# Clustered attention with a token-mixing MLP: the order and the staging of the weight sums are changed

## The chip, the cores and the metric

The kernel runs on one core of a Trainium2 chip. The metric is the device time of one execution in microseconds (us). Five engines work side by side and are ordered by semaphores: PE (TensorE: matmuls and their weight loads), DVE (VectorE), ACT (ScalarE), POOL (GpSimd) and SP (SyncE, which here only issues DMAs). Each engine runs its instructions strictly in the order of the program: one that waits holds all that stand behind it on that engine. ACT issues some DMAs too. Matmul results are written to PSUM banks; everything else is in SBUF or in DRAM.

## The reference

```
q_assign = argmax(normalised q . normalised centroids);  k_assign likewise
scores   = where(q_assign == k_assign, q k^T / 8, -1e9);  attn = softmax(scores) v
x  = attn, heads joined                      # [4, 768, 512]
u  = x + (x^T U V)^T                         # rank-32 mix over the 768 tokens
out = u + relu(u w_ch1) w_ch2                # 512 -> 2048 -> 512, for each batch
```

There are 4 batches, 8 heads, 768 tokens, 64 values a head. U, V, w_ch1 and w_ch2 come as float64; the kernel gets their bits as int64.

## The kernel before

**Attention.** 16 items (4 batches by 4 pairs of heads) go through a software pipeline of 12 steps an item. `M0` is the step after the last item, where the MLP begins; times below are in steps after M0.

**The plan.** All work is cut into small functions (`gemm1`, `join`'s caller `load_weights`, `recover`, `store_sum`, ...). `at(time, fn, args)` puts each call into a list under a hand-chosen time; the list is sorted by it and run once, at build time. So a time is no time of the chip: it sets only the order in which instructions stand on each engine.

**The MLP in two ways.** Batch 0 is done directly, as two halves of 384 tokens (`nh = 2`) of 16 steps each: in step f, `gemm1` (12 matmuls, L598 to L600) multiplies by one 128-column slice of w1, `after_gemm1` (ACT L606, DVE L607) applies relu and splits the result into a high and a low float32r part, and `gemm2` (9 matmuls, L617 to L619) multiplies by the matching slice of w2, half a step to a step later. Every operand is held as a high and a low part, and three products stand for one. Batches 1 to 3 are done from step 32 on by a scheme with seven instead of eight block products (`seven1` L800 to L802, `seven2` L876 to L878). It needs, for w1 and w2 of each group, three blocks A11, A12, A22 and four sums of blocks S1 to S4. They are made once, beside batch 0, put into DRAM (`wc`) and fetched from there (`fetch_w1` L771, `fetch_w2` L783).

**Loading weights.** The weights are in four groups g of 512 columns, each with 4 pieces of w1 and 4 of w2, 128x512 each. Groups 0 and 1 are loaded during the attention. For groups 2 and 3 one piece is loaded in each of the steps 0 to 15: `fetch` (L151, a DMA of 512 KB on ACT's queue, two buffers), `upper` (ACT L159), `join` (DVE L169, L170, L172: the float32 is put together from the bits, in a PSUM bank of the pool that also serves gemm1 and the mix), then the high part (ACT L190) and the low part (DVE L191).

**A turn.** One turn makes the four sums of w1 or w2 of one group. `recover` adds high and low of a block again (ACT L659 copies the low part into the bank `ps_r`, DVE L660 adds the high part), `combine` (POOL L665 to L671) forms the sums, `split_high` (ACT L676) and `split_low` (POOL L680) split them, and `store_sum` (SP L684, L685) stores both parts. There are eight turns, in the order of the groups 0 to 3, 3.1 steps apart from step 3 on; the last begins at 26.3. `store_block` (SP L643) stores the plain blocks.

**Tokens.** u of a batch goes through DRAM (`u_scr`, stored in `mix_v`, L552). `fetch_u` and `turn_u` (PE transposes L587, ACT L589, DVE L590) bring the halves of batch 0, `fetch_half` (L738) and `turn_half` (L743) those of batch 1; `u_sums` and `u_halves` make the sums of token blocks for the seven products. `mix_u` (L533), `mix_sum` (L540 to L543) and `mix_v` (L549, L550) are the rank-32 mix; that of batch 3 lies in the first steps of the MLP.

Of the kernel before, what the change touches and what calls it, by code (L numbers as in the profile page):

```python
# [89 lines left out]
    "mix_u":    ( 18.88,  18.35,  18.48,  16.57),  # L90
    "mix_sum":  ( 19.11,   19.1,  19.15,  18.35),
    "mix_v":    (  20.5,   20.4,  20.68,  19.42),
}
# [24 lines left out]
def clustered_attention_moe(ctx: ExitStack, tc: tile.TileContext, qk, v, cen, moe_U, moe_V, w1, w2, out):  # L118
# [26 lines left out]

    def fetch(srcs, n, queue=nc.sync):

        step = srcs[0].shape[0]
        rw = raw.tile([P, 512], I64, name="rw")[0:step * len(srcs), 0:n]
        for i, src in enumerate(srcs):  # L150
            queue.dma_start(out=rw[i * step:(i + 1) * step], in_=src)  # L151
        return rw
# [9 lines left out]
    def join(rw, g, in_bank=False):  # L162


        r, n = rw.shape
        low = rw.bitcast(I32).rearrange("p (n two) -> p n two", two=2)[:, :, 0]
        b = work("ps_t").bitcast(I32)[0:r, 0:n]
        t = b if in_bank else raw.tile([P, 512], I32, name="rw_t")[0:r, 0:n]
        nc.vector.tensor_scalar(b, g, 3, None, op0=ALU.logical_shift_left)  # L169
        nc.vector.scalar_tensor_tensor(out=b, in0=g, scalar=-0x80000000, in1=b,  # L170
                                       op0=ALU.bitwise_and, op1=ALU.bitwise_or)
        nc.vector.scalar_tensor_tensor(out=t, in0=low, scalar=29, in1=b,  # L172
                                       op0=ALU.logical_shift_right, op1=ALU.bitwise_or)
        return rw, g, t
# [3 lines left out]
    def load_weights(g, step, stage):  # L178

        k, i = divmod(step, 4)  # L180
        if stage == 0:
            parts[g, step] = fetch([(w1, w2)[k][g, :, i, :]], 512, nc.scalar if g > 1 else nc.sync)
        elif stage == 1:
            parts[g, step] = upper(parts[g, step])
        elif stage == 2:
            parts[g, step] = join(*parts[g, step], g > 1)
        else:
            w = parts.pop((g, step))[2].bitcast(F32)
            hi, lo = wg[g][2 * k][:, i, :], wg[g][2 * k + 1][:, i, :]
            nc.scalar.copy(hi, w)  # L190
            (nc.vector if g > 1 or g == 1 and step in (1, 2, 3, 5) else nc.gpsimd).tensor_sub(lo, w, hi)  # L191

# [448 lines left out]
    def store_block(k, g, name, part):  # L641

        nc.sync.dma_start(out=wc[k][g][:, :, slot[k][name], part * 256:part * 256 + 256],  # L643
                          in_=blocks(k, g, part)[name].bitcast(F32))

    def temps(n):
        at = 3072 * (n % 2 == 0 or n > 5)
        return [pool["f"][:, at + 512 * j:at + 512 * j + 512].rearrange("p (a n) -> p a n", a=2) for j in range(4)]

    def high_of(n, j):  # L650
        f = pool["f"]
        places = [f[:, 5120:5632], f[:, 5632:6144], *pool["o"], f[:, 2048:2560], f[:, 2560:3072]]
# [37 lines left out]
    w1s = [w0.rearrange("p k i n -> p (k i n)")[:, 3584 * k:3584 * k + 3584] for k in range(2)]  # L690
    spare, count = [], {"bank": 0, "f": 0, "o": 0}

# [6 lines left out]
    def open_sevens():  # L699
# [6 lines left out]
        pool["st"] = rows.tile([P, HT, DM], F32, name="st", tag="R")  # L706
        ring = []
        for _ in range(2):
            ring += pieces(raw.tile([P, 512], I64, name="rw").bitcast(F32)[:, 0:768], HS)
        ring += [raw.tile([P, 512], F32, name="rw_g")[:, 0:HS] for _ in range(2)]  # L710
# [26 lines left out]
    def fetch_half(b, h):  # L737
        nc.sync.dma_start(out=pool["st"], in_=u_scr[b][:, h * HT:(h + 1) * HT, :])  # L738

# [268 lines left out]
    for b, (t_u, t_sum, t_v) in enumerate(zip(*mixes.values())):  # L1008
# [16 lines left out]
    at(M0 + 8.05, open_weights)  # L1025
# [10 lines left out]

    for n_, (g, k) in enumerate((g, k) for g in range(NG) for k in range(2)):
        c = M0 + (3 + 3.1 * n_ if n_ < 7 else 26.3)
        for r in range(4):
            at(c + 0.4 * r, recover, n_, k, g, r)  # L1040
            at(c + (0.9, 1.4, 1.75, 2.1)[r], combine, n_, r)
            at(c + (1.9, 2.25, 2.6, 2.8)[r], split_high, n_, r)
            at(c + (2.4, 2.7, 3.0, 3.3)[r], split_low, n_, r)
            at(c + (2.8, 3.1, 3.4, 3.7)[r], store_sum, n_, k, g, r)
# [96 lines left out]
```

## Time and profile before

| what | value |
|---|---|
| median of 3 runs | 1006.9 us (1006.17 to 1006.93) |
| the profiled execution | 1010.74 us, span 1008.9 us |
| mean granted clock of TensorE | 0.982 |
| PE busy | 954.8 us, 95% of the span |
| DVE busy | 713.3 us, 71% |
| POOL busy | 613.7 us, 61% |
| ACT busy | 471.9 us, 47% |
| first matmul of batch 0's MLP (step 0) | 466.9 us |
| its second half (step 16) | 557.4 us |
| first of the seven products (step 32) | 634.4 us |

Busy times are of the whole span; shares in single stages differ. The view of waits says for an engine which line waited for what (line waiting <- engine and line that released it), with the total, the number and the longest. Rows of a timeline have the start, the length, the engine, the line, the operation, what it writes and reads, and in brackets the idle time ahead of it with its releaser. `SPq` and `ACTq` are DMA issues. In the view of windows, the last four columns are the granted clock, the mean share of the 16 DMA engines that was busy, and GB/s.

### The profile page before, as it was taken

Reading aid. Unit: us, or ns where it says so; the run is one execution under the profiler, and the core shown is the slowest. Engines: PE = TensorE matmul, PEld = TensorE weight load, DVE = VectorE, ACT = ScalarE, POOL = GpSimd, SP = SyncE. Lnnn points to the kernel's source line nnn. Section 1 sums busy time; section 2 is a strip of 40 time slices with the busy share of each in tenths; the row PEclk is TensorE's granted clock in tenths of the full one; section 3 lists DMA queues with packets and bytes.
Section 4 is the critical chain, followed back from the end, with each engine's and each line's share of the span. In section 5 each row is a group of like instructions: output and inputs, shape, how many; then the busy total and the mean of one; then the engine's idle time right before and its main releaser. Section 6 shows DMA issues by size and latency. Waiting matters only on the chain. (4 is left out here: it accounts for less than half of the span.)

```text
span 1008.9 us, 15372 instructions
## 1 busy us (share of the span) xinstructions
PE 954.8 (95%) x5368; PEld 779.5 (77%) x5368; DVE 713.3 (71%) x1315; ACT 471.9 (47%) x837; POOL 613.7 (61%) x460
## 2 busy tenths in 40 slices
PE   6899999999999999988989998899999999999997
PEld 3565665676666766656767888799999999999997
DVE  5797776777787767676788523765788766877766
ACT  4454555565555545464455534443444433453330
POOL 5466676889678867753356845732357723866333
PEclk8899999999999999989999998999999999999999
DMA  6754653656575645346476994876667696676744
GB/s 182 193 130 118 163 147 94 201 155 158 144 227 155 152 116 147 98 132 231 142 234 229 312 350 180 315 275 241 256 237 274 221 377 239 227 280 252 261 147 146
DMA packets 76158, 205.28 MB, mean 203 GB/s; under 512 B 8561, under 2 KB 42865, under 8 KB 71217
## 3 DMA queue, kind: packets, MB, share of 16 engines
q1 hardware_dynamic: 73392, 195.82, 60.5%
q10 hardware_dynamic: 2688, 8.49, 2.7%
q8 instruction: 42, 0.69, 0.3%
q14 instruction: 36, 0.29, 0.1%
HBM read 131.07 MB, written 41.94 MB: 171 GB/s over the span
## 5 line engine op out<-in xcount | busy, mean ns | idle before, releaser
L442 DVE TENSOR_REDUCE m<-ps_max 128x1 f32<-128x384 f32 x384 | 195.3, 548 | 82.9 <-PE ps_max L440 81.2
L479 POOL TENSOR_TENSOR T<-T,pr 128x768 f32<-128x768 f32 x120 | 225.9, 1882 | 45.8 <-ACT pr L469 19.5
L469 ACT ACTIVATE pr<-st 128x768 f32<-128x768 f32 x192 | 154.6, 813 | 85.9 <-PE st L466 69.2
L440 PE MATMUL ps_max<-arena 128*128 128x384 f32 x384 | 127.1, 382 | 6.6 <-DVE oh L356 2.5
L487 PE MATMUL o_ps<-pr,vt 128*64 128x384 f32 x768 | 132.6, 495 | 0.1
L464 PE MATMUL st<-arena 128*128 128x384 f32 x384 | 105.2, 355 | 2.1 <-ACT pr L469 2.1
L440 PEld LDWEIGHTS ps_max<-arena 128*128 128x128 f32 x384 | 70.9, 193 | 45.1 <-issue 21.4
L487 PEld LDWEIGHTS o_ps<-pr,vt 128*64 128x64 f32 x768 | 52.9, 138 | 66.6 <-issue 60.3
L466 PE MATMUL st<-arena 97*128 97x384 f32 x384 | 99.6, 341 | 4.5 <-DMA arena<-mT 2.7
L479 POOL TENSOR_TENSOR T<-pr 128x768 f32<-128x768 f32 x30 | 56.5, 1883 | 65.1 <-ACT pr L469 65.1
L464 PEld LDWEIGHTS st<-arena 128*128 128x128 f32 x384 | 66.2, 190 | 18.1 <-issue 9.9
L466 PEld LDWEIGHTS st<-arena 97*128 97x128 f32 x384 | 70.3, 190 | 6.5 <-issue 4.6
L800 PE MATMUL ps_p<-arena,w 128*128 128x384 f32 x186 | 62.7, 337 | 2.8 <-DMA w<-wc 2.8
L491 ACT COPY os<-o_ps 128x384 f32<-128x384 f32 x32 | 15.4, 480 | 105.1 <-PE o_ps L487 105.1
L801 PE MATMUL ps_p<-arena,w 128*128 128x384 f32 x186 | 62.8, 338 | 0.2 <-POOL arena L767 0.2
L802 PE MATMUL ps_p<-arena,w 128*128 128x384 f32 x186 | 62.5, 336 | 0.0
L800 PE MATMUL ps_q<-arena,w 128*128 128x384 f32 x150 | 50.5, 337 | 0.0
L801 PE MATMUL ps_q<-arena,w 128*128 128x384 f32 x150 | 50.3, 336 | 0.0
L802 PE MATMUL ps_q<-arena,w 128*128 128x384 f32 x150 | 50.3, 335 | 0.0
L380 POOL TENSOR_TENSOR arena<-R,arena 128x768 fp32r<-128x768 f32 x18 | 34.5, 1921 | 13.6 <-ACT arena L375 8.0
L665 POOL TENSOR_TENSOR f<-f 128x512 f32<-128x512 f32 x8 | 10.3, 1294 | 53.1 <-DVE f L660 53.1
L607 DVE SCALAR_TENSOR_TENSOR hx<-ps_h,hx 128x384 fp32r<-128x384 f32 x32 | 17.7, 554 | 29.3 <-ACT hx L606 29.2
(527 smaller groups left out, 2454.6 us busy)
## 6 DMA issues: line engine op xcount, KB each, us to landing
w<-wc SPq DMA_DIRECT2D x24, 1024.0 KB
w<-wc SPq DMA_DIRECT2D x24, 768.0 KB
arena<-wc SPq DMA_DIRECT2D x20, 768.0 KB
wc<-f SPq DMA_DIRECT2D x52, 256.0 KB
R<-in_qk SPq DMA_DIRECT2D x32, 384.0 KB
arena<-arena SPq DMA_DIRECT2D x32, 384.0 KB
arena<-arena SPq DMA_DIRECT2D x64, 192.0 KB
arena<-wc SPq DMA_DIRECT2D x10, 1024.0 KB
```

The costliest lines, as they stand in the source:

```text
L380: eng.tensor_sub(part(X2[i % 3], 0, h), live["R", i][:, 2 * h:2 * h + 2].rearrange("p j q -> p (j q)"), part(X1[i % 3], 0, h))
L440: nc.tensor.matmul(ps[:, 0:HS], x1[:, 0, g // 2, g % 2, t * P:(t + 1) * P], x1[:, 1, h, g % 2, :], start=True, stop=True)
L442: nc.vector.reduce_max(live["m2", i][:, h, u:u + 1], ps[:, 0:HS], axis=AX.X)
L464: nc.tensor.matmul(st[:, j, 0:HS], x1[:, 1, hk, j, ks], x1[:, 0, h, j, :], start=True, stop=False)
L466: nc.tensor.matmul(st[:, j, 0:HS], x2[0:97, 1, hk, j, ks], x2[0:97, 0, h, j, :], start=False, stop=True)
L469: nc.scalar.activation(pr, st[:, :, 0:HS], AF.Exp, scale=SCALE)
L479: eng.tensor_add(T, live["p", i, h, 0] if c == 1 else T, live["p", i, h, c])
L487: nc.tensor.matmul(o_ps[64 * j:64 * j + 64, 0:HS], vv[:, c, j, :], pr[:, j, :], start=(c == 0), stop=(c == NT - 1))
L607: nc.vector.scalar_tensor_tensor(out=hl, in0=ps[:, 0:HS], scalar=0.0, in1=hh, op0=ALU.max, op1=ALU.subtract)
L800: nc.tensor.matmul(ps, w[:, 0, k], u[:, 0, k], start=(k == 0), stop=False)
L801: nc.tensor.matmul(ps, w[:, 0, k], u[:, 1, k], start=False, stop=False)
L802: nc.tensor.matmul(ps, w[:, 1, k], u[:, 0, k], start=False, stop=(k == 1))
```

## The change

- The order of the turns becomes groups 2, 3, 0, 1 (`turns_of`). For the first four, `recover` is left out: a new fifth stage of `load_weights`, `keep_joined`, copies the joined weights on ACT from the bank straight into the turn's scratch in `f`. Turns begin at 2.8, 6.8, 10.8, 14.8, 17.5, 20.0, 22.7 and 26.4; of the last, everything after `recover` comes 5.9 steps later.
- The stages of a load are spread: the fetch 2.6 steps ahead of the step (for the first two pieces 4.6), `upper` 1.45, `join` 0.45, high part 0.02, low part 0.0, `keep_joined` 0.53 behind. All fetches go on SP's queue. Every third piece goes into a third buffer in `f`.
- `join` of these groups uses the bank `ps_r`, one buffer, instead of the shared pool.
- `mix_sum` of batch 3 comes 0.7 steps earlier; its `mix_v` one tile each 0.45 steps instead of three at once. `turn_u(0)` is spread from step -7 on, `turn_half(1, h)` comes 3.8 and 2.0 steps earlier, `u_sums` of batch 1 1.1. `fetch_half(1, 1)` goes on ACT's queue, at 22.5 instead of 25.6. B11's subtraction in `u_halves` of batch 1 moves from POOL to DVE.
- Blocks of groups 2 and 3 are stored from step 4.6 on instead of 15.5. `fetch_w1` of the first two pairs moves from 23 and 26 to 24.5 and 28, `fetch_w2` to 30 through 32.2.

```
-    "mix_sum":  ( 19.11,   19.1,  19.15,  18.35),
-    "mix_v":    (  20.5,   20.4,  20.68,  19.42),
+    "mix_sum":  ( 19.11,   19.1,  19.15,  17.65),
+    "mix_v":    (  20.5,   20.4,  20.68,  18.42),
...
-    "g2":   ( -1.25,      0,    0.4,    0.7),
-    "g3":   (  6.75,      8,    8.4,    8.7),
+    "g2":   (  -2.6,  -1.45,  -0.45,  -0.02,   0.0,   0.53),
+    "g3":   (   5.4,   6.55,   7.55,   7.98,   8.0,   8.53),
...
-        b = work("ps_t").bitcast(I32)[0:r, 0:n]
+        b = (pool["y"].tile([P, 512], F32, name="ps_r") if in_bank else work("ps_t")).bitcast(I32)[0:r, 0:n]
...
-            parts[g, step] = fetch([(w1, w2)[k][g, :, i, :]], 512, nc.scalar if g > 1 else nc.sync)
+            spare_rw = None
+            if g > 1 and (8 * g + step) % 3 == 0:
+                spare_rw = pool["f"][:, 2048:3072].bitcast(I64)
+            parts[g, step] = fetch([(w1, w2)[k][g, :, i, :]], 512, nc.sync, spare_rw)
...
-            w = parts.pop((g, step))[2].bitcast(F32)
             hi, lo = wg[g][2 * k][:, i, :], wg[g][2 * k + 1][:, i, :]
-            nc.scalar.copy(hi, w)
-            (nc.vector if g > 1 or g == 1 and step in (1, 2, 3, 5) else nc.gpsimd).tensor_sub(lo, w, hi)
+            if stage == 3:
+                w = parts[g, step][2].bitcast(F32)
+                nc.scalar.copy(hi, w)
+            if stage == 5:
+                keep_joined(turns_of.index((g, k)), i, parts.pop((g, step))[2].bitcast(F32))
+            if stage == 4 or stage == 3 and g < 2:
+                w = parts[g, step][2].bitcast(F32)
+                eng = nc.vector if g > 1 or g == 1 and step in (1, 2, 3, 5) else nc.gpsimd
+                eng.tensor_sub(lo, w, hi)
...
+    turns_of = [(2, 0), (2, 1), (3, 0), (3, 1), (0, 0), (0, 1), (1, 0), (1, 1)]
+    def keep_joined(n, i, w):
+        at = 3072 * (n % 2 == 0)
+        f = pool["f"][:, at:at + 2048].rearrange("p (c k a n) -> p c k a n", c=2, k=2, a=2)
+        to = f[:, i // 2, :, i % 2] if n % 2 else f[:, :, 1 - i // 2, i % 2]
+        nc.scalar.copy(to, w.rearrange("p (c n) -> p c n", c=2))
...
-        return places[count["o"] % (6 if n < 6 else 4)].rearrange("p (a n) -> p a n", a=2)
+        return places[count["o"] % (4 if n < 7 else 2)].rearrange("p (a n) -> p a n", a=2)
...
-        nc.sync.dma_start(out=pool["st"], in_=u_scr[b][:, h * HT:(h + 1) * HT, :])
+        (nc.scalar if b == 1 and h else nc.sync).dma_start(out=pool["st"], in_=u_scr[b][:, h * HT:(h + 1) * HT, :])
...
-            at(o + t_v + (t if b < B - 1 else t // HT), mix_v, b, t)
+            at(o + t_v + (t if b < B - 1 else 0.45 * t), mix_v, b, t)
...
-                at(step + pace * k + (M0 if g else 0), load_weights, g, k, stage)
+                ahead = 2 if g == 2 and stage == 0 and k < 2 else 0
+                at(step + pace * k + (M0 if g else 0) - ahead, load_weights, g, k, stage)
...
-            at(m + (-4.5 + d if i else -1.52), turn_u, i, d)
+            at(m + (-4.5 + d if i else -7 + 0.6 * d), turn_u, i, d)
...
-        c = M0 + (3 + 3.1 * n_ if n_ < 7 else 26.3)
+        c = M0 + (2.8, 6.8, 10.8, 14.8, 17.5, 20.0, 22.7, 26.4)[n_]
+        if n_ > 3:
+            for r in range(4):
+                at(c + 0.3 * r, recover, n_, k, g, r)
+        wait = 5.9 if n_ == 7 else 0
...
+                since = (95, 142, M0 - 9, M0 - 2.5, M0 + 4.6, M0 + 10.6, M0 + 16.4, M0 + 19.7)[2 * g + k]
+                at(since + (6, 0.9, 1, 0.55)[g] * x, store_block, k, g, name, half)
...
-            fetched, turns = (o - 13.9, o - 6.4), (o - 7.7, o - 5.4)
+            fetched, turns = (o - 13.9, o - 9.5), (o - 11.5, o - 7.4)
...
-            at(M0 + 23 + 3 * K, fetch_w1, K, s0, s1)
-            at(M0 + (30.5 + 0.5 * K if s0 == 0 else 31.8 + 0.1 * K), fetch_w2, K, *range(s0, s1))
+            at(M0 + 24.5 + 3.5 * K, fetch_w1, K, s0, s1)
+            at(M0 + (30 + 0.7 * K if s0 == 0 else 31.5 + 0.7 * K), fetch_w2, K, *range(s0, s1))
```

More of the change, by code (lines that the diff above doesn't have):

```diff
@@ L144, in clustered_attention_moe, with fetch @@
     u_scr = [dram.tile([P, NT, DM], F32, name=f"u_scr{b}") for b in range(B)]
-    def fetch(srcs, n, queue=nc.sync):
+    def fetch(srcs, n, queue=nc.sync, rw=None):
         step = srcs[0].shape[0]
-        rw = raw.tile([P, 512], I64, name="rw")[0:step * len(srcs), 0:n]
+        if rw is None:
+            rw = raw.tile([P, 512], I64, name="rw")[0:step * len(srcs), 0:n]
         for i, src in enumerate(srcs):
@@ L644, in store_block @@
                           in_=blocks(k, g, part)[name].bitcast(F32))
+    turns_of = [(2, 0), (2, 1), (3, 0), (3, 1), (0, 0), (0, 1), (1, 0), (1, 1)]
[4 more added lines that the diff above has]
+        nc.scalar.copy(to, w.rearrange("p (c n) -> p c n", c=2))
     def temps(n):
         at = 3072 * (n % 2 == 0 or n > 5)
-        return [pool["f"][:, at + 512 * j:at + 512 * j + 512].rearrange("p (a n) -> p a n", a=2) for j in range(4)]
+        x = pieces(pool["f"][:, at:at + 2048], 512) if n != 5 else pool["wide"]
+        return [x[j].rearrange("p (a n) -> p a n", a=2)
+                for j in ((1, 0, 3, 2) if n % 2 else range(4))]
     def high_of(n, j):
         f = pool["f"]
-        places = [f[:, 5120:5632], f[:, 5632:6144], *pool["o"], f[:, 2048:2560], f[:, 2560:3072]]
+        places = [f[:, 5120:5632], f[:, 5632:6144], *pool["o"]]
         count["o"] += 1
-        return places[count["o"] % (6 if n < 6 else 4)].rearrange("p (a n) -> p a n", a=2)
+        return places[count["o"] % (4 if n < 7 else 2)].rearrange("p (a n) -> p a n", a=2)
     def recover(n, k, g, j):
@@ L690, in clustered_attention_moe @@
     w1s = [w0.rearrange("p k i n -> p (k i n)")[:, 3584 * k:3584 * k + 3584] for k in range(2)]
-    spare, count = [], {"bank": 0, "f": 0, "o": 0}
+    spare, count = [], {"bank": 0, "f": 3, "o": 0}
     def pieces(x, n):
@@ L706, in open_sevens @@
         pool["st"] = rows.tile([P, HT, DM], F32, name="st", tag="R")
-        ring = []
+        ring, pool["wide"] = [], []
         for _ in range(2):
-            ring += pieces(raw.tile([P, 512], I64, name="rw").bitcast(F32)[:, 0:768], HS)
+            x = raw.tile([P, 512], I64, name="rw").bitcast(F32)
+            ring += pieces(x[:, 0:768], HS)
+            pool["wide"] += pieces(x, 512)
         ring += [raw.tile([P, 512], F32, name="rw_g")[:, 0:HS] for _ in range(2)]
@@ L721, in open_right @@
         pool["acc"] = {key: acc[k // 2][:, k % 2] for k, key in enumerate((B11, T1, T3, T2))}
-        count["f"] = 13
+        count["f"] = 16
         pool["ring"] += pieces(right.tile([P, 4 * HS], F32, name="ring"), HS)
@@ L761, in u_halves @@
             nc.scalar.copy(hi, u_block(b, key))
-            nc.gpsimd.tensor_sub(lo, u_block(b, key), hi)
+            (nc.vector if b == 1 and key == B11 else nc.gpsimd).tensor_sub(lo, u_block(b, key), hi)
         else:
@@ L1021, in clustered_attention_moe @@
             for k in range(8):
-                at(step + pace * k + (M0 if g else 0), load_weights, g, k, stage)
+                ahead = 2 if g == 2 and stage == 0 and k < 2 else 0
+                at(step + pace * k + (M0 if g else 0) - ahead, load_weights, g, k, stage)
     at(M0 - 0.75, open_mlp)
-    at(M0 + 8.05, open_weights)
+    at(M0 + 7.9, open_weights)
     for i in range(nh):
@@ L1035, in clustered_attention_moe @@
         at(m + (16.35 if i == 0 else 16.47), finish, i)
-    for n_, (g, k) in enumerate((g, k) for g in range(NG) for k in range(2)):
-        c = M0 + (3 + 3.1 * n_ if n_ < 7 else 26.3)
-        for r in range(4):
[L1040 to L1044, printed above, removed]
+    for n_, (g, k) in enumerate(turns_of):
+        c = M0 + (2.8, 6.8, 10.8, 14.8, 17.5, 20.0, 22.7, 26.4)[n_]
[3 more added lines that the diff above has]
+        wait = 5.9 if n_ == 7 else 0
+        for r in range(4):
+            at(c + wait + (0.9, 1.4, 1.75, 2.1)[r], combine, n_, r)
+            at(c + wait + (1.9, 2.25, *((4.0, 4.5) if wait else (2.6, 2.8)))[r], split_high, n_, r)
+            at(c + wait + (2.4, 2.7, *((4.4, 4.9) if wait else (3.0, 3.3)))[r], split_low, n_, r)
+            at(c + wait + (2.8, 3.05, *((4.8, 5.3) if wait else (3.4, 3.7)))[r], store_sum, n_, k, g, r)
         for r, name in enumerate(("A11", "A12", "A22")):
@@ L1067, in clustered_attention_moe @@
             for r in range(2):
-                at((o - 4.9 if b > 1 else o - 3.9) + (k + 0.5 * r) * (1 if b > 1 else 0.8), u_sums, b, key, r)
+                at((o - 4.9 if b > 1 else o - 5) + (k + 0.5 * r) * (1 if b > 1 else 0.8), u_sums, b, key, r)
         for key, when_ in ((B11, -4.95), (T1, -4.2), (B21, -3.7), (T2, -3.2), (B22, -2.7), (T3, -2.2), (T4, -1.2)):
```

3 lines of the change are left out of this document (removed).

## The prediction

> **What bounds the kernel now.** I read the page first.
>
> ```profile
> span 1008.9 us, 15372 instructions
> ```
>
> The profiled execution took 1010.74 us, its span 1008.9; the median of the runs shown is 1006.9, 0.4% less. I work out a difference within the span and take it from the median. A change under 0.2%, 2 us, cannot be told from none here.
>
> Second, the windows by stage, cut at the first matmul of L598 (466.9), at the second half of batch 0 (557.4) and at the first seven-product matmul (634.4). Columns: stretch, length, then PE, PEld, DVE, ACT and POOL busy.
>
> ```profile
> 0.00:466.90 466.90, 441.42 (x2560) 292.41 (x2560) 345.28 (x673) 251.90 (x381) 335.00 (x230) 0.98 0.57 154
> 466.90:557.40 90.50, 78.18 (x376) 63.54 (x377) 67.97 (x112) 45.68 (x89) 41.77 (x33) 0.98 0.61 199
> 557.40:634.40 77.00, 72.62 (x361) 65.06 (x360) 30.48 (x45) 33.11 (x65) 49.38 (x38) 0.96 0.82 278
> 634.40:1008.90 374.50, 362.54 (x2075) 358.49 (x2073) 269.52 (x488) 141.17 (x304) 187.56 (x162) 0.99 0.68 251
> ```
>
> PE is the bound everywhere and no other engine is full for long. The change touches the second and third row and the seam to the fourth. I call the second row the loading stretch (16 steps of gemm1 and gemm2, with groups 2 and 3 loaded beside them) and the third the second half. A step there is (72.6 busy − 2.8 lost to the clock, below − 24 token transposes at 0.13, below) / 16 = 4.2 us.
>
> Third, what PE waited for from 466 to 660: total, times, longest.
>
> ```profile
> PE ps_h L549 <- DVE xt L550: 4.8, 2, 2.6
> PE y L619 <- DVE hx L607: 3.6, 4, 1.6
> PE ps_uT L743 <- DMA st<-u_scr: 3.3, 1, 3.3
> PE y L617 <- ACT hx L606: 2.9, 2, 1.8
> PE ps_p L800 <- DMA w<-wc: 2.8, 1, 2.8
> PE y L618 <- DVE w2l L191: 1.4, 2, 1.0
> ```
>
> Their sum is 18.8. Fourth, the granted clock (third column from the right) behind the long ones.
>
> ```profile
> 515.00:525.00 10.00, 8.26 (x33) 7.40 (x34) 8.28 (x14) 5.25 (x10) 6.73 (x6) 0.83 0.75 254
> 605.00:610.00 5.00, 1.72 (x7) 1.75 (x8) 0.00 (x0) 0.81 (x2) 0.00 (x0) 0.70 0.98 384
> 610.00:615.00 5.00, 5.00 (x19) 4.61 (x18) 0.96 (x2) 1.14 (x3) 1.27 (x1) 0.61 0.93 331
> 655.00:660.00 5.00, 5.00 (x21) 5.00 (x22) 1.22 (x4) 1.70 (x4) 1.48 (x2) 0.68 0.80 335
> ```
>
> Length times (1 − clock) is the work lost: 1.7 in the first; in the next two 0.5 × 1.72 + 1.95 = 2.8 (the rest fell on idle time); 1.6 in the last. 6.1 in all, so 24.9 us are to be had.
>
> **The change part by part.** *Sums from joined weights.* The first four turns (groups 2 and 3) skip `recover`: 16 ACT copies and 16 DVE adds leave the loading stretch, and 16 ACT copies of the same size (`keep_joined`) come in.
>
> ```profile
> 487.19 0.60 ACT L659 COPY ps_r<-w 128x512 f32<-128x512 f32 x1
> ```
> ```profile
> 487.90 0.69 DVE L660 TENSOR_TENSOR f<-ps_r,w 128x512 f32<-128x512 f32 x1 [0.43 <-ACT ps_r L659]
> ```
>
> ACT: 16 × 0.60 out, 16 × 0.60 in, nothing. DVE: 16 × 0.69 = 11.0 out, so 68.0 becomes 57.0. Turns 4 to 7 keep their recovers, now in the second half, where DVE is busy for 30 of 77: hidden; without that cover, 16 × 0.69 again.
>
> *Stages a step apart, own bank.* One load's path is now one chain: join (three DVE operations) into `ps_r`, L190 on ACT, L191 on DVE, and the next join must wait for `keep_joined`, which frees the only bank.
>
> ```profile
> 478.60 0.67 DVE L169 TENSOR_SCALAR ps_t<-rw_g 128x512 int32<-128x512 int32 x1
> 479.31 0.70 DVE L170 SCALAR_TENSOR_TENSOR ps_t<-rw_g,ps_t 128x512 int32<-128x512 int32 x1
> 480.04 0.69 DVE L172 SCALAR_TENSOR_TENSOR ps_t<-rw,ps_t 128x512 int32<-128x512 int32 x1
> 480.64 0.55 DVE L607 SCALAR_TENSOR_TENSOR hx<-ps_h,hx 128x384 fp32r<-128x384 f32 x1
> 481.39 0.69 DVE L191 TENSOR_TENSOR arena<-ps_t,arena 128x512 fp32r<-128x512 f32 x1 [0.19 <-ACT arena L190]
> ```
> ```profile
> 480.77 0.59 ACT L190 CAST arena<-ps_t 128x512 fp32r<-128x512 f32 x1 [3.71 <-DVE ps_t L172]
> 480.83 0.33 ACTq L151 DMA_DIRECT2D rw<-in_w  x1
> 481.25 0.67 ACT L159 ACTIVATE rw_g<-rw 128x512 f32<-128x512 f32 x1
> 481.82 0.48 ACT L606 ACTIVATE hx<-ps_h 128x384 fp32r<-128x384 f32 x1
> ```
>
> The order by time within a step is L606/L607, keep, L159 of the load after next, join, L190, L191. DVE's chain: L607 0.55 + join 2.13 (478.60 to 480.73) + wait for L190 0.66 + L191 0.69 + about 0.1 for keep, which runs beside L607, = 4.1. Over 16 steps 66. The other DVE work there (six adds of `mix_v` at 0.69 by the L660 row, the same shape; two of `normalise`, four of `turn_u`, one of `mix_sum` at 0.55 to 0.69) is 8.5, of which some 2.5 fit into the waits for L190: 72 in all. PE's own work is 78.2 − 1.7 = 76.5. So PE should stay the bound, narrowly; L607 has a whole step before gemm2 needs it. I leave 2.4 of the waits standing.
>
> *What goes with it.* `join` leaves the shared banks and `mix_v` comes 0.45 steps apart instead of three at once: the 4.8 at L549 (full banks behind DVE's joins) and its clock, 1.7, go. Splits come a step before gemm2 instead of half a step: the 1.4 at L618. `mix_sum` moves 0.7 steps ahead, so that L543 stands behind a join and not ahead of it: with the emptier DVE the 3.6 at L619.
>
> *Earlier loads.* Of the 2.9 at L617, 1.8 is the start: ACT held for 5.35 by the first load, L606 behind it.
>
> ```profile
> 472.64 0.66 ACT L159 ACTIVATE rw_g<-rw 128x512 f32<-128x512 f32 x1 [5.35 <-DMA rw<-in_w]
> ```
>
> The first two loads now go out 3.35 steps earlier and the others 1.35, into three buffers. All move from ACT's queue (16 × 0.33 saved there) to SP's, behind stores; that is the first rival. SP itself waits at the first two until `join` of group 1 has freed a buffer; behind them are only stores that nobody needs for 100 us: nothing. The third buffer's first load waits until the attention's last sums have read that memory; behind it is the fourth load, needed two steps later: nothing.
>
> *Token turns.* `turn_u(0)` moves from just before gemm1 to between the scores of the last item.
>
> ```profile
> 465.08 1.53 PE L587 MATMUL ps_uT<-ident,u 128*128 128x128 f32 x12
> ```
> ```profile
> 455.30:462.10 6.80, 6.47 (x38) 5.08 (x40) 4.75 (x8) 6.41 (x10) 3.51 (x4) 1.00 0.87 305
> 570.00:610.00 40.00, 36.69 (x188) 33.09 (x187) 9.96 (x16) 14.79 (x30) 21.35 (x17) 0.96 1.05 362
> ```
>
> That saves 1.8 (465.08 to 466.9) and puts 1.5 on PE and four ACT copies at about 0.5 into 455 to 462, where ACT is busy for 6.4 of 6.8 and paces the scores: −1.8 to +2.0 net, I take 0.
>
> *Second token fetch.* `fetch_half(1, 1)` went out on SP behind stores; PE waited 3.3 for it and lost 2.8 to the clock.
>
> ```profile
> 601.98 0.61 SPq L738 DMA_DIRECT2D st<-u_scr  x1
> ```
>  Now it is on ACT's queue, 2.1 steps = 8.8 us before its turn instead of 1.0, in a calmer stretch. From 570 to 610 (second row above, last columns) the DMA engines were full, share 1.05, 362 GB/s. After the change I count, from step 16 to 24.6, three turns of stores (8 × 262 KB each), twelve blocks, an output half and two token halves: 11.8 MB in 36 us, 328 GB/s. The old fetch took from 602.0 to 608.3 (PE's 1.72 busy before 610 starts there) in the full stretch, so 8.8 should do; 0.5 left. The blocks of groups 2 and 3, which filled that stretch, now go from step 4.6 to 22.5 instead of 15.5 to 28, into a loading stretch whose DMA share was 0.61.
>
> *Last turn and first fetches.* The combine and splits of turn 7 go 5.9 steps later, into the seven-product stage; `fetch_w2` no longer stands behind its stores.
>
> ```profile
> 636.78 2.21 SPq L783 DMA_DIRECT2D arena<-wc  x4
> 639.05 0.53 SPq L783 DMA_DIRECT2D w2l<-wc  x1
> 639.67 1.61 SPq L626 DMA_DIRECT2D out_y<-u  x3
> 642.20 0.33 SPq L771 DMA_DIRECT2D w<-wc  x1
> ```
>
> These 3.7 MB of w2 and 0.8 MB of output ahead of L771 are why PE waited 2.8 until about 655 and lost 1.6. They can now leave at step 30, before 630. With the turn gone, ACT no longer waits there for POOL: the other 1.1 at L617. POOL gets 8 operations at 1.30 after 637.
>
> ```profile
> 491.46 1.30 POOL L665 TENSOR_TENSOR f<-f 128x512 f32<-128x512 f32 x1 [23.12 <-DVE f L660]
> ```
>
> 10.4 us, where POOL is half idle (187.6 of 374.5) and seven2, which needs POOL's h_low, starts only 5.25 steps in. Turn 7's stores now stand in SP's queue between the w1 fetches of the fourth and fifth unit, which are needed some 3 steps later; its third and fourth split reuse two buffers and could hold ACT, with L823 and L852 behind, until a store has landed. 0 to 2 in all, I take 0.5. `u_sums` a step earlier and B11's subtraction on DVE fall where DVE is idle for 46 of 77 us: nothing.
>
> *Sum.* 24.9, less 2.4 + 0.5 + 0.5 of waits and one more half-clock period of 1.6: 19.9. **1006.9 − 19.9 = 987.0 us.**
>
> That period is charged because the clock row at 655 stands behind a wait of only 2.8. The Trainium skill, TensorE: Matmul & The Clock Gate, Part 1, lets the clock halve only after an idle window of about 3.4 us; by it no wait here would cost clock, the trace disagrees (0.68 behind 2.8), and without the 1.6 the sum would be 985.4.
>
> **The rivals.** *Slower: a load held on SP.* SP issues in order, and a load now stands behind `store_sum`, which waits for POOL's `split_low`.
>
> ```profile
> SPq L685 <- POOL f L680: 21.6, 18, 7.5
> ```
> ```profile
> 521.13 0.33 ACTq L151 DMA_DIRECT2D rw<-in_w  x1
> ...
> 528.56 0.66 ACT L159 ACTIVATE rw_g<-rw 128x512 f32<-128x512 f32 x1 [1.38 <-DMA rw<-in_w]
> ```
>
> With eight stores in flight a load took 7.4 us to L159. A load is issued 1.15 steps = 4.8 ahead, and the join before covers 2.1 more. A hold as long as SP's longest (7.5) would cost 7.5 + 7.4 − 6.9 = 8 a turn: ACT stands at L159 with L606 behind it. Over the three turns of the loading stretch that is 24, 4 more than the gain: 1011. It decides from 6 us of hold a turn. Against it: the mean hold is 21.6/18 = 1.2, and POOL has 10.4 of work in 16.7 us a turn there.
>
> *The chain binds.* If nothing overlaps between the engines, a step is L606 0.48 + keep 0.60 + join 2.13 + L190 0.66 + L191 0.69 + a split's 0.6 = 5.2; 16 of them are 83 and with 3 of the rest 86, 9.5 over PE's 76.5: 996.
>
> *The token fetch stays late.* 3.3 + 2.8 are not saved: 993. For it: the load above started on ACT's queue and still had to wait for SP's stores. The Trainium skill, DMA: Bandwidth & Descriptors, Issuing engines are not separate DMA queues, says that changing the issuing engine saves only issue time; that row agrees. Against it: 8.8 us against 6.3.
>
> *It only moves waits.* Keep and recover cost ACT the same, the waits come back elsewhere: 1006.
>
> **How the numbers follow.** Forecast 0.48; chain 0.17; late fetch 0.17; no change 0.05; held loads 0.13. Faster 0.48 + 0.17 + 0.17 = 0.82, same 0.05, slower 0.13. The low end takes all 24.9 and 1.5 of the token turns: 980. The high end has the chain and the late fetch together (987 + 9.5 + 6.1 = 1002.6): 1002.
>
> **What would show it.** Right: the rows L549, L743 and L800 gone from PE's waits; the loading stretch near 79, the second half near 70; no clock under 0.9 between 500 and 660 but for one period; DVE below 60 in the loading stretch. Wrong: ACT idle at L159 behind a DMA (held loads); DVE idle at L191 behind L190 and PE at L619 (chain); PE at L743 behind `st` (late fetch); PE idle after 640 behind POOL.

## The result, and the profile after

The changed kernel takes 982.2 us (median of 4 runs, 981.05 to 982.48), the kernel before beside it on the same chip 1006.5 (1005.56 to 1006.93). The ratio is 0.9757, 95% interval 0.974 to 0.9774: 24.4 us less, where 19.9 were forecast. Medians and ratios here and below leave out two executions far outside all others, one of 3209 us (e12) and one of 2162 us (before, beside e1 to e4).

The page of after. PE's share of the span rose from 95% to 97%.

```profile
span 980.7 us, 15364 instructions
...
PE 946.5 (97%) x5368; PEld 776.7 (79%) x5368; DVE 701.1 (71%) x1300; ACT 472.5 (48%) x837; POOL 611.7 (62%) x459
```

The windows of after, cut at the same four places as before (first matmul of gemm1, second half, first of the seven products). Columns as there: stretch, length, PE, PEld, DVE, ACT, POOL busy, granted clock, DMA share, GB/s.

```profile
0.00:467.70 467.70, 443.35 (x2559) 294.07 (x2559) 345.90 (x675) 252.20 (x380) 334.86 (x229) 0.97 0.57 154
467.70:540.70 73.00, 72.90 (x378) 62.74 (x377) 57.35 (x94) 42.28 (x81) 33.92 (x26) 1.00 0.82 273
540.70:610.70 70.00, 69.92 (x362) 62.89 (x362) 31.67 (x47) 35.86 (x70) 53.25 (x42) 1.00 0.87 305
610.70:980.70 370.00, 360.33 (x2074) 356.95 (x2072) 266.23 (x486) 142.13 (x306) 189.68 (x163) 0.99 0.68 248
```

Compare row by row: the start is 0.8 longer (467.7 against 466.9), the loading stretch 17.5 shorter (73.0 against 90.5), the second half 7.0 (70.0 against 77.0), the seven products 4.5 (370.0 against 374.5). In the middle rows PE is busy for 72.90 of 73.00 and 69.92 of 70.00 at a clock of 1.00. The view of PE's waits from 466 to 640, which takes in the first 29 us of the seven products, has no row at all; the six of before, 18.8 us, are gone. DVE in the loading stretch went from 67.97 to 57.35.

The four differences sum to 28.2, the span's own (1008.9 − 980.7). The medians give 24.4. The profiled execution of before took 1010.74, 4.2 above the median of its runs here, that of after 982.48, 0.3 above its own. In which row of before these 4 us lie, no view tells; they may be part of the 17.5. The granted clocks on record give a hint. Of 30 other executions of before, those under 1007 us had a mean clock of 0.984 to 0.988, those above 1009 one of 0.978 to 0.984, and the profiled one had 0.982; 0.003 of 1007 is 3 us. So some of the 6.1 that the profile of before lost to the clock is likely its own, and not in the medians.

A step now takes 73.0 / 16 = 4.6 us. How near DVE's chain comes to that can be read from after's timeline of DVE, one step of the loading stretch (start, length, engine, line, and in brackets the idle time ahead with its releaser).

```profile
510.02 0.55 DVE L617 SCALAR_TENSOR_TENSOR hx<-ps_h,hx 128x384 fp32r<-128x384 f32 x1
510.81 0.69 DVE L170 TENSOR_SCALAR ps_r<-rw_g 128x512 int32<-128x512 int32 x1 [0.23 <-ACT f L663]
511.53 0.70 DVE L171 SCALAR_TENSOR_TENSOR ps_r<-rw_g,ps_r 128x512 int32<-128x512 int32 x1
512.26 0.69 DVE L173 SCALAR_TENSOR_TENSOR ps_r<-rw,ps_r 128x512 int32<-128x512 int32 x1
513.61 0.69 DVE L201 TENSOR_TENSOR w1l<-ps_r,w1h 128x512 fp32r<-128x512 f32 x1 [0.65 <-ACT w1h L195]
```

From L617 to the end of L201 it is 4.28, of which DVE idles 0.23 behind `keep_joined` (L663) and 0.65 behind the high part (L195). The forecast had 4.1 for this chain. The waits are there, and PE does not see them.

### The profile page after: what moved, and what is told of

It reads as the page before. It is cut to its first block, busy times and chain, and to the rows that moved or that the text cites. A ratio compares the mean times of both kernels' runs of the same rounds, so it can differ in the third digit from the quotient of the medians.

```text
span 980.7 us, 15364 instructions
## 1 busy us (share of the span) xinstructions
PE 946.5 (97%) x5368; PEld 776.7 (79%) x5368; DVE 701.1 (71%) x1300; ACT 472.5 (48%) x837; POOL 611.7 (62%) x459
## 4 chain that ended last, share of the span: by engine, by line
PE 81%; DVE 9%; DMA 4%; ACT 3%; issue 2%; POOL 1%; SPq 0%; DVEq 0%; ACTq 0%; POOLq 0%
PE o_ps L497 13%; PE ps_max L450 8%; PE st L474 6%; PE st L476 6%; PE ps_p L825 3%; PE ps_p L824 3%; PE ps_p L823 3%; PE ps_q L899 3%; PE ps_q L824 3%; PE ps_q L825 3%; PE ps_q L823 3%; PE ps_q L901 3%; PE ps_q L900 3%; PE ps_p L899 2%; PE ps_p L901 2%; PE ps_p L900 2%
## 5 line engine op out<-in xcount | busy, mean ns | idle before, releaser
L452 DVE TENSOR_REDUCE m<-ps_max 128x1 f32<-128x384 f32 x384 | 195.3, 547 | 84.1 <-PE ps_max L450 82.6
L823 PE MATMUL ps_p<-arena,w 128*128 128x384 f32 x186 | 62.2, 334 | 0.0
L823 PE MATMUL ps_q<-arena,w 128*128 128x384 f32 x150 | 50.1, 334 | 0.0
L824 PEld LDWEIGHTS ps_p<-arena,w 128*128 128x128 f32 x186 | 34.9, 188 | 0.1
L823 PEld LDWEIGHTS ps_p<-arena,w 128*128 128x128 f32 x186 | 34.9, 188 | 0.1
```

The source lines that it names most:

```text
L452: nc.vector.reduce_max(live["m2", i][:, h, u:u + 1], ps[:, 0:HS], axis=AX.X)
L823: nc.tensor.matmul(ps, w[:, 0, k], u[:, 0, k], start=(k == 0), stop=False)
L824: nc.tensor.matmul(ps, w[:, 0, k], u[:, 1, k], start=False, stop=False)
```

## The experiments

Each kernel is the changed one with one edit. Theory A is the prediction's own reason for a part, theory B a rival for that part; each text on record says what the two expect. Lengths are those of the profiled execution, cut as above (after: 467.7, 73.0, 70.0).

| kernel | median us | ratio to before, 95% | start | loading | second half |
|---|---|---|---|---|---|
| after | 982.16 | 0.9757 [0.974, 0.9774] | 467.7 | 73.0 | 70.0 |
| e1, recover all | 995.02 | 0.9874 [0.9847, 0.9902] | 466.7 | 84.1 | 72.3 |
| e2, shared bank | 988.35 | 0.9802 [0.9775, 0.9829] | 467.8 | 78.8 | 69.6 |
| e3, low part twice | 987.61 | 0.9797 [0.977, 0.9823] | 466.8 | 78.1 | 70.9 |
| e4, mix as before | 983.20 | 0.9757 [0.973, 0.9784] | 467.7 | 74.9 | 69.6 |
| e5, token fetch late | 981.22 | 0.9733 [0.9718, 0.9749] | 466.2 | 72.7 | 70.9 |
| e6, last turn early | 989.26 | 0.9802 [0.9782, 0.9822] | 468.2 | 72.5 | 77.8 |
| e7, blocks late | 984.40 | 0.9765 [0.9747, 0.9782] | 467.9 | 72.6 | 73.7 |
| e8, loads late | 988.29 | 0.9804 [0.9786, 0.9822] | 465.4 | 79.6 | 70.1 |
| e9, loads on ACT | 982.78 | 0.9750 [0.9726, 0.9773] | 465.5 | 75.5 | 69.6 |
| e10, turn_u as before | 980.01 | 0.9722 [0.9699, 0.9745] | 466.0 | 72.6 | 70.0 |
| e11, last turn early, b | 982.62 | 0.9747 [0.9724, 0.9771] | 465.6 | 72.7 | 72.2 |
| e12, no lead | 982.51 | 0.9756 [0.9729, 0.9782] | 467.8 | 72.9 | 69.9 |

The 982.51 of e12 is the median of five runs. A price below has two ends: the difference of the medians from 982.2, and the difference of the ratios times 1007. They differ by up to 2.6 us, because the batches had other runs of before beside them (medians 1007.1 for e1 to e4, 1008.2 for e5 to e8, 1008.1 for the rest).

### e1: the first four turns recover their weights again

```
-                keep_joined(turns_of.index((g, k)), i, parts.pop((g, step))[2].bitcast(F32))
+                parts.pop((g, step))
...
-        if n_ > 3:
-            for r in range(4):
-                at(c + 0.3 * r, recover, n_, k, g, r)
+        for r in range(4):
+            at(c + (0.3 * r if n_ > 3 else (0.25, 0.5, 1.25, 1.5)[r]), recover, n_, k, g, r)
```

> The changed kernel, but the first four turns recover their blocks from high and low parts again instead of taking the joined weights (the recovers stand between a load's low part and the next join, since they share the bank). 16 ACT copies leave, 16 ACT copies and 16 DVE adds come. Theory A (the loading stretch is short because DVE's chain through the one bank just fits a step): the chain grows by a copy and an add, 1.3 us, on average each step, 5.3 against a step of 4.6: the loading stretch 8 to 15 us longer, time 990 to 997, PE waiting at gemm2 for hx. Theory B (the order of the turns and the spreading do it, the joined sums nothing by themselves): 982 to 984.

Measured 995.0, 11.8 to 12.9 more. PE's waits from 466 to 640 (total, times, longest):

```profile
PE y L627 <- ACT hx L616: 6.6, 5, 2.0
PE ps_h L559 <- DVE x L553: 0.9, 1, 0.9
PE y L629 <- DVE hx L617: 0.2, 1, 0.2
```

Its windows, the whole loading stretch and the place of the longest wait:

```profile
466.70:550.80 84.10, 77.40 (x378) 63.22 (x377) 65.47 (x106) 40.99 (x79) 32.35 (x25) 0.98 0.73 238
537.00:543.00 6.00, 5.21 (x17) 4.03 (x18) 4.30 (x7) 4.06 (x10) 5.60 (x5) 0.72 0.42 150
```

DVE is at 65.47, 8.1 above after. Theory A holds: with the adds back on DVE and the copies on ACT inside the loads, relu comes late and gemm2 (L627) waits for it. The clock fell once (0.72 over 6 us is 1.7 lost). About half the gain of the change hangs on this part. It is a combined price: 16 adds and copies, their place in the order, and the one bank that the recovers here share with the joins.

### e2: the join back in the shared banks

```
-        b = (pool["y"].tile([P, 512], F32, name="ps_r") if in_bank else work("ps_t")).bitcast(I32)[0:r, 0:n]
+        b = work("ps_t").bitcast(I32)[0:r, 0:n]
```

> The changed kernel, but join writes into the pool of four banks that gemm1 and the mix use. Theory A (the 4.8 us at the mix matmuls were full banks): a bank is held for some 4 us a step, PE waits again at mix_v, 2 to 5 us, time 984 to 987. Theory B (with the mix spread and DVE emptier the banks no longer matter): 981 to 983.

Measured 988.4, 4.5 to 6.2 more, and more than theory A expects. PE's waits in the loading stretch (one more row has 0.2), and its window:

```profile
PE ps_h L608 <- DVE xt L560: 1.5, 3, 0.5
PE ps_h L608 <- ACT sums L511: 1.3, 1, 1.3
PE ps_h L608 <- DVE hx L617: 1.2, 2, 1.0
```
```profile
467.80:546.60 78.80, 74.56 (x378) 62.71 (x377) 58.09 (x95) 42.97 (x83) 33.88 (x26) 1.00 0.77 254
```

gemm1's first matmul (L608) now finds no free bank. Each wait names another releaser, whoever last held that bank, as one would expect of a pool that is too small. The bank matters, though with `mix_v` spread out the waits stand at gemm1 and not at the mix, where before had them.

### e3: the low part of groups 2 and 3 made twice

```
+                if g > 1:
+                    eng.tensor_sub(lo, w, hi)
```

> The changed kernel with the low-part subtraction of groups 2 and 3 done twice, the second time over the first with the same result: 16 more DVE operations of 0.69 us, one in each step's chain. Theory A (chain of 4.1 us in a step of 4.6): the chain is 4.8, over 16 steps 11 us more of which 2 to 5 are hidden: 988 to 991. Theory B (DVE is busy for only 57 of 73 us there, so it has room): 982 to 984.

This kernel does the same subtraction twice, 16 × 0.69 = 11.0 more on DVE, in the middle of the chain. Measured 987.6, 4.0 to 5.4 more. PE's waits from 466 to 552, and the window of the loading stretch:

```profile
PE y L631 <- DVE hx L619: 0.9, 3, 0.3
PE y L629 <- ACT hx L618: 0.7, 2, 0.4
PE y L630 <- DVE w2l L203: 0.4, 1, 0.4
```
```profile
466.80:544.90 78.10, 76.12 (x379) 61.89 (x378) 67.22 (x108) 42.39 (x81) 34.02 (x26) 1.00 0.77 256
```

Of 11.0 on the chain 5.1 came through to the stretch, so some 6 of room were there: the chain of waits between ACT and DVE is next behind PE, as the prediction had it ("narrowly"), but it does not bind. Theory A holds, at the low end of its 988 to 991. PE shows only 2.0 of idle time for these 5.1; where the rest went is said below.

### e4: the mix of the last batch at its old times

```
-    "mix_sum":  ( 19.11,   19.1,  19.15,  17.65),
-    "mix_v":    (  20.5,   20.4,  20.68,  18.42),
+    "mix_sum":  ( 19.11,   19.1,  19.15,  18.35),
+    "mix_v":    (  20.5,   20.4,  20.68,  19.42),
...
-            at(o + t_v + (t if b < B - 1 else 0.45 * t), mix_v, b, t)
+            at(o + t_v + (t if b < B - 1 else t // HT), mix_v, b, t)
```

> The changed kernel with mix_sum of batch 3 0.7 steps later and its mix_v three at once again. Theory A (spreading removed the wait at the mix matmuls): PE waits again at L559 and, for mix_sum, at gemm2, 3 to 6 us with a fall of the clock, 985 to 988. Theory B (the own bank alone removed it: three mix tiles and one of gemm1 fill four banks, and DVE is free): 982 to 983.

Measured 983.2, 0 to 1.0 more, within the measurement. One wait came back in the loading stretch, of the 4.8 that before had at the same pool:

```profile
PE ps_h L608 <- DVE xt L560: 1.8, 2, 1.3
```

Theory B holds here: the joins' own bank ends most of that wait without the spread, and spreading the mix is worth 1 at most beside it. Nothing came back at gemm2, so the move of `mix_sum` by itself is not what ended the 3.6 at L619.

### e5: the token fetch late, and on SP

```
-        (nc.scalar if b == 1 and h else nc.sync).dma_start(out=pool["st"], in_=u_scr[b][:, h * HT:(h + 1) * HT, :])
+        nc.sync.dma_start(out=pool["st"], in_=u_scr[b][:, h * HT:(h + 1) * HT, :])
...
-            fetched, turns = (o - 13.9, o - 9.5), (o - 11.5, o - 7.4)
+            fetched, turns = (o - 13.9, o - 6.4), (o - 7.7, o - 5.4)
...
-                at((o - 4.9 if b > 1 else o - 5) + (k + 0.5 * r) * (1 if b > 1 else 0.8), u_sums, b, key, r)
+                at((o - 4.9 if b > 1 else o - 3.9) + (k + 0.5 * r) * (1 if b > 1 else 0.8), u_sums, b, key, r)
```

> The changed kernel with the token halves of batch 1 at their old times: the second half is fetched on SP's queue 1.0 step (4.2 us) before its turn, and u_sums follow at their old times. Theory A (the lead removed the wait): the fetch takes 6 us where the DMA engines are full, PE waits 2 to 3.5 us at the token transposes and loses 1.6 to 2.8 to the clock: 986 to 988. Theory B (the emptier queue removed it, the lead is spare): 982 to 983.

Measured 981.2, not more than after. The wait of before, 3.3, is down to a third by itself (PE's waits in the second half), and no clock fell behind it:

```profile
PE ps_uT L766 <- DMA st<-u_scr: 1.1, 1, 1.1
```

Theory B holds nearly: a fetch one step ahead comes almost in time. Of the 2.3 that the wait is shorter, the fetch itself is 1.1 (6.3 from issue to PE's start in before, 601.98 to 608.28; 5.2 here, 582.23 to 587.45), in a stretch with a DMA share of 0.82 (582.0 to 588.5) against 1.05. The other 1.2 is the time from the issue to PE's arrival, 4.2 against 3.0. That the blocks' stores make both differences is argued, not shown. The lead and the queue earn nothing that can be measured beside that.

### e6 and e11: the last turn not held back

```
-        wait = 5.9 if n_ == 7 else 0
+        wait = 0
```

> The changed kernel without the 5.9 steps of delay: combine, splits and stores of the last turn follow its recover at once, beside u_halves and ahead of fetch_w2 on SP. Theory A (POOL cannot do the turn and u_halves in that time, ACT waits in split_high and the fetches of w2 stand behind the stores): 1 us at gemm2 and 2.8 + 1.6 at the first fetch of w1 come back, 986 to 988. Theory B (the other order of the turns or the calmer DMA queues removed both): 982 to 983.

In e6 the third and fourth split of that turn write into the two buffers before their first contents are stored, so two of its stored high parts hold other values. Measured 989.3, 4.5 to 7.1 more, above both ranges. ACT's long wait (590 to 612), and the windows around what it did to PE:

```profile
ACT f L697 <- POOL f L701: 8.5, 2, 5.3
```
```profile
605.00:610.00 5.00, 0.71 (x2) 0.50 (x2) 0.57 (x2) 2.43 (x5) 5.00 (x5) 0.85 0.42 139
610.00:615.00 5.00, 5.00 (x14) 4.18 (x13) 1.65 (x2) 2.15 (x6) 5.00 (x5) 0.50 1.03 292
```

`split_high` on ACT waits for POOL to be done with one of only two buffers, relu is queued behind it, PE stops for 4.3 and comes back at half clock. That mixes two things, the early turn and its two buffers, so e11 puts the third and fourth split behind the first stores and leaves the turn early:

```
-        wait = 5.9 if n_ == 7 else 0
+        wait = 0.01 if n_ == 7 else 0
```

> The changed kernel with the last turn 5.9 steps earlier, as in the run with that edit, but its third and fourth split kept behind the stores of the first two. Theory A (POOL cannot do the turn and u_halves together, ACT waits in split_high with the relu behind it): PE waits at gemm2 for 3 to 5 us and loses 1.6 to 2.8 to the clock, 985 to 990. Theory B (the loss of that run came from its two buffers, a split waiting for a store): 982 to 984.

Measured 982.6, the same as after. PE's waits from 538 to 630:

```profile
PE y L629 <- DVE hx L617: 1.6, 3, 0.7
PE ps_p L823 <- DMA w<-wc: 0.6, 1, 0.6
```

Theory B holds. The second half is 2.2 longer in the profile and the fetch of w1 (L823) late by 0.6, but the median does not show it. e6's loss came from the order of splits over two buffers, not from the turn's place.

### e7: the blocks of groups 2 and 3 stored late

```
-                since = (95, 142, M0 - 9, M0 - 2.5, M0 + 4.6, M0 + 10.6, M0 + 16.4, M0 + 19.7)[2 * g + k]
-                at(since + (6, 0.9, 1, 0.55)[g] * x, store_block, k, g, name, half)
+                since = (95, 142, M0 - 9, M0 - 2.5, M0 + 15.5, M0 + 18.8, M0 + 22.1, M0 + 25.4)[2 * g + k]
+                at(since + (6, 0.9, 0.55, 0.55)[g] * x, store_block, k, g, name, half)
```

> The changed kernel with the plain blocks of groups 2 and 3 stored from step 15.5 to 28 as before, 6.3 MB put back into the second half. Theory A (the spread stores are what lets the token fetch and the fetches of w1 and w2 land in time): waits for DMAs at the token transposes or at seven1, each with a fall of the clock, 985 to 992. Theory B (the leads are long enough for a full queue): 982 to 984.

Measured 984.4, 0.8 to 2.2 more, between the two ranges; its interval (up from 0.9747) overlaps that of after (up to 0.9774). In the profile the second half is 3.7 longer. DVE's waits from 580 to 612, and one row of its timeline:

```profile
DVE f L681 <- DMA wc<-f: 8.2, 2, 5.5
DVE hx L617 <- ACT hx L616: 7.0, 1, 7.0
```
```profile
591.86 0.69 DVE L681 TENSOR_TENSOR f<-ps_r,arena 128x512 f32<-128x512 f32 x1 [5.51 <-DMA wc<-f]
```

With twelve more blocks on the DMA engines here, a stored sum leaves its buffer late, `recover` (L681) waits 5.5 for that, and what stands behind it on DVE waits too; PE had 3.1 in three waits at gemm2. I had reckoned the blocks only as company of the token fetch; they act through the turns' buffers.

### e8, e12 and e9: the loads

e8 takes away the third buffer and the lead of the first two loads, e12 the lead alone, e9 puts the loads on ACT's queue.

```
-            if g > 1 and (8 * g + step) % 3 == 0:
+            if False:
...
-                ahead = 2 if g == 2 and stage == 0 and k < 2 else 0
+                ahead = 0
```

> The changed kernel with two load buffers instead of three and without the two steps that the first two loads go ahead. Theory A (the first loads' lead removed the 1.8 us at the first gemm2; later loads have 1.15 steps either way): 982.5 to 985. Theory B (held loads, the rival of the prediction: with two buffers SP waits for a join before each load, L160 waits for the DMA and holds L616 on ACT): 986 to 995.

```
-                ahead = 2 if g == 2 and stage == 0 and k < 2 else 0
+                ahead = 0
```

> The changed kernel with three load buffers but the first two loads not ahead by two steps. Theory A (in the run with two buffers and no lead the third buffer's loss made the 6 us, the lead nothing, since its first six steps were as long as with it): 981 to 983. Theory B (the lead removes the wait at the first gemm2): 984 to 986, all of it in the first two steps.

```
-            parts[g, step] = fetch([(w1, w2)[k][g, :, i, :]], 512, nc.sync, spare_rw)
+            parts[g, step] = fetch([(w1, w2)[k][g, :, i, :]], 512, nc.scalar if g > 1 else nc.sync, spare_rw)
```

> The changed kernel with the loads of groups 2 and 3 issued on ACT's queue again, at the same times and with three buffers. Theory A (the engines that move the data are the same; what counts is the buffer and the lead): 981 to 984, ACT has the 16 issues of 0.33 us to spare. Theory B (on ACT a load that waits for its buffer holds the relu L616, on SP it only holds stores): ACT stands for the 22.9 us that SP now waits for buffers, or part of it, 985 to 995.

e8 took 988.3, 4.7 to 6.1 more; e12 982.5 and e9 982.8, both the same as after. So beside the third buffer the lead earns nothing, and e8's loss comes from the buffer, alone or with the lead; two buffers with the lead were not run. Waits of e8 in its loading stretch, one engine a fence: SP, ACT, PE.

```profile
SPq L152 <- DVE ps_r L173: 44.3, 12, 7.4
```
```profile
ACT rw_g L160 <- DMA rw<-in_w: 30.8, 14, 4.9
```
```profile
PE y L627 <- ACT hx L616: 4.2, 5, 1.4
```

SP's and ACT's same waits in after:

```profile
SPq L152 <- DVE ps_r L173: 22.9, 10, 3.9
```
```profile
ACT rw_g L160 <- DMA f<-in_w: 3.6, 3, 1.5
...
ACT rw_g L160 <- DMA rw<-in_w: 2.8, 1, 2.8
```

With two buffers the load waits on SP until the join has freed one (44.3 against 22.9), goes out too late, and ACT stands at L160 for 30.8 (after: 6.4) with relu behind it. That is the rival "a load held on SP" in its mechanism, held by its own buffer and not by `store_sum`. In e9 the queue is another and the median the same, though in its profile the loading stretch is 2.5 longer, with 1.7 of waits at L627 behind L616, and the start 2.2 shorter. The Trainium skill, DMA: Bandwidth & Descriptors, Issuing engines are not separate DMA queues, says that the issuing engine saves only issue time; e9 and e5 agree, at 982.8 and 981.2 against 982.2.

### e10: turn_u(0) back at its old place

```
-            at(m + (-4.5 + d if i else -7 + 0.6 * d), turn_u, i, d)
+            at(m + (-4.5 + d if i else -1.52), turn_u, i, d)
```

> The changed kernel with the token turns of the first half just before gemm1 again. Theory A (ACT paces the stretch into which they were moved, so that the move gains nothing): 981 to 983. Theory B (the PE time of 1.5 us and the wait behind it are saved by the move): 983.5 to 985.

Measured 980.0 (979.33 to 981.12), 2.2 to 3.5 less, below both ranges. The intervals overlap (up to 0.9745 here, from 0.974 in after), so it is the fastest version seen and not a settled gain. What is settled is that the move saves nothing: of the prediction's −1.8 to +2.0, the part below 0 is out. Starts with the move ran from 465.4 (e8) to 468.2 (e6), and 466.0 without lies among them.

## Why the prediction was right

**The mechanism held.** PE was taken for the bound, and its waits and falls of clock for all that was to be had. After, PE idles 0.2 of 143 us there. The loading stretch lost 17.5 where the steps gave 10.9 (4.8 + 1.7 + 3.6 + 1.4 + 1.8 − 2.4), the second half 7.0 where they gave 6.7 (3.3 + 2.8 + 1.1 − 0.5), the seven products 4.5 where they gave 3.9 (2.8 + 1.6 − 0.5). DVE's 57.0 came out at 57.35. Of the signs named, the loading stretch "near 79" did not come true: it was 73.0.

**Where the miss lies.** By the medians it is 4.5, and the 5.0 held back in the sum (2.4 + 0.5 + 0.5 of waits and 1.6 of clock) would cover it alone: none of the four came. By the spans 28.2 came, 3.3 more than the 24.9 that were to be had; for that the next term is needed, and the longer profiled execution of before has its part in it.

**The term that was mis-sized** is the one by which PE's own work in the loading stretch is 78.2 − 1.7 = 76.5, with 2.4 of waits left over it. It was 72.9 with as many matmuls, and nothing was left over. Busy time is not work: a stop also lengthens what is booked as busy. Here are five matmuls of after without a stop, the last of gemm1 and the first of gemm2, then the same five places in e8 with one stop, both at full clock.

```profile
511.57 0.33 PE L610 MATMUL ps_h<-arena 128*128 128x384 f32 x1
511.75 0.39 PE L627 MATMUL y<-arena,hx 128*128 128x512 f32 x1
511.98 0.40 PE L628 MATMUL y<-w2l,hx 128*128 128x512 f32 x1
512.21 0.40 PE L629 MATMUL y<-arena,hx 128*128 128x512 f32 x1
512.45 0.39 PE L627 MATMUL y<-arena,hx 128*128 128x512 f32 x1
```
```profile
530.52 0.34 PE L610 MATMUL ps_h<-arena,w1l 128*128 128x384 f32 x1
532.25 0.50 PE L627 MATMUL y<-w2h,hx 128*128 128x512 f32 x1 [1.39 <-ACT hx L616]
532.59 0.49 PE L628 MATMUL y<-w2l,hx 128*128 128x512 f32 x1
533.05 0.50 PE L629 MATMUL y<-w2h,hx 128*128 128x512 f32 x1
533.39 0.40 PE L627 MATMUL y<-w2h,hx 128*128 128x512 f32 x1
```

In after the gemm2 matmuls start 0.23 apart and last 0.39 by the profile, so each overlaps the next by 0.16; the step from L610 to L627 overlaps as much. From the first to the fifth start it is 0.88 in after and 2.87 in e8: 1.99 more, of which the view of waits shows 1.39. The rest is booked as busy. The broken overlap is 0.16. The matmul behind the stop lasts 0.50, and the next starts 0.34 later instead of 0.23. And L629 starts 0.46 behind L628 with no idle time in the row, and the next again 0.34 behind: a delay shorter than the overlap shows no wait at all.

The 6.6 that I missed (17.5 − 10.9) are 2.4 that I left standing, 3.6 of such busy time (76.5 − 72.9) and 0.6 of idle time in waits of 0.3 and less that the terms leave out (12.3 idle by the window of before, less 11.6 in the terms and 0.1 of after). So a stop cost more than the view of waits shows, but by no fixed factor: (17.5 − 1.7) / 11.9 = 1.3 in before, 6.6 / 4.2 = 1.6 in e8, 5.8 / 4.2 = 1.4 in e2, 1.9 / 1.8 = 1.1 in e4, and 5.1 / 2.0 = 2.6 in e3, where most delays were short. How much of before's 17.5 is its longer profiled execution is open.

**The charged half-clock period** of 1.6 did not come: no clock below 1.00 stands between 460 and 660. One of 3.4 stands at 89.4, in the attention, where nothing was changed; eight of the twelve experiments have none there. It belongs to the execution, and with the 0.8 of the start it is not the change's.

**Costs put at nothing** held in that PE has no wait from them: keep for recover on ACT (busy for 42.28 against 45.68), the recovers moved into the second half, SP's waits at the first loads.

**The rivals.** The chain needs some 6 us more work to bind (e3). Held loads are real and came with one buffer less and no lead (e8). The late token fetch did not happen, but not for the reason that I gave: 8.8 us of lead was hardly needed (e5), and the stretch was no calmer. After's timeline of ACT has the issue, its windows the ten microseconds behind it, with a DMA share of 1.04 (1.05 before):

```profile
569.51 0.35 ACTq L761 DMA_DIRECT2D st<-u_scr  x1
```
```profile
570.00:580.00 10.00, 10.00 (x53) 8.91 (x51) 4.32 (x7) 4.84 (x9) 9.76 (x9) 1.00 1.04 337
```

**The sum is right, its parts are not additive.** Undone alone, the joined sums cost 12 to 13, the bank 4.5 to 6, the third buffer (with the lead) 5 to 6, the early blocks 1 to 2 at most; the mix's spread, the lead of the loads, the fetch's lead and queue, and `turn_u`'s move cost nothing that can be measured. It looks as if the bank and the mix's spread end the same wait, and the blocks' new place and the token fetch's lead another; no run undoes two of them together, so this is argued. Not undone at all were the order of the turns, the earlier splits, and the places of `fetch_w1` and `fetch_w2`. What ended the 1.4 at L618 and the 2.8 and 1.6 at the first fetch of w1 is therefore argued too; the early turn of e11 brought back 0.6 of the latter.

## What to carry to other kernels

Where one engine is the bound and stops often for a short time, its busy time is no measure of its work: take the work from a stretch in which it never stops. A stop costs more than the view of waits shows (here 0.27 and more beyond its idle time), and a delay shorter than the overlap of two matmuls shows as no wait. When a transfer is late, look first at what frees its buffer and whose place in an in-order queue it holds: here two load buffers instead of three cost 5 to 6 us, and another queue or an earlier issue earned nothing that could be measured. A change of many parts should be undone part by part, as half of these earned nothing beside the others.

## What the runs showed of the hardware

In these runs the clock fell by a fixed grid, and not by the length of a wait alone. The records of the granted clock change at whole multiples of 3.413 us from each other in every run. Two waits of before for the same bank, in its timeline:

```profile
508.95 0.51 PE L549 MATMUL ps_h<-x,v 96*128 96x512 f32 x1 [2.63 <-DVE xt L550]
...
516.65 0.50 PE L549 MATMUL ps_h<-x,v 96*128 96x512 f32 x1 [2.17 <-DVE xt L550]
```

The longer one cost no clock, the shorter one did, at 518.29. Counted back from there, the grid has cells from 504.64 to 508.05, to 511.47, and from 514.88 to 518.29: the wait of 2.63 (506.32 to 508.95) is cut into 1.73 and 0.90, while 1.77 of the 2.17 (514.48 to 516.65) lie in one cell, which had 1.86 of idle time in all. The windows of before for these cells and the one behind (second number PE busy, third from the right the clock):

```profile
504.64:508.05 3.41, 1.68 (x8) 1.02 (x6) 2.46 (x5) 1.88 (x4) 1.19 (x1) 1.00 0.97 309
508.05:511.47 3.42, 2.44 (x12) 2.12 (x13) 3.42 (x7) 0.78 (x2) 0.15 (x1) 1.00 0.57 158
514.88:518.29 3.41, 1.54 (x7) 1.23 (x8) 3.38 (x7) 2.18 (x4) 2.29 (x3) 1.00 0.30 61
518.29:521.71 3.42, 3.42 (x12) 3.14 (x11) 3.19 (x7) 1.07 (x3) 2.01 (x2) 0.50 0.99 400
```

Over all runs, between 460 and the last matmuls, the clock fell from full behind each cell with 1.86 us idle or more (1.86, 2.07, 2.13, 2.77, 3.39) and behind none with 1.73 or less. At half clock less was enough to keep it there: a cell with 1.24 idle (607.04 to 610.45 in before) and one with 0.90 (e6) were followed by another at half. So about half a cell is enough to lose full clock, and the same wait costs 1.7 us of work or none by where it falls. The Trainium skill, TensorE: Matmul & The Clock Gate, Part 1, has a free-running window of 3413 ns, which agrees, and lets the clock halve after an idle one; here a cell with 1.86 of 3.41 idle sufficed. In the attention, with its small matmuls, it fell behind cells with less (1.07 us idle, from 86.03 to 89.44 in after), so the bound is one for dense matmuls.
